# Infini-attention block, one core: a fifth stack slot, earlier stack loads, and a group's mixing, rounding and output products two steps later

## The chip, the core and the metric

The kernel runs on one core of a Trainium2 chip. Its engines work side by side, each on its own list of instructions in a fixed order: PE (TensorE, products; its weight loads are listed as PEld), DVE (VectorE), ACT (ScalarE), POOL (GpSimd) and SP (SyncE, which here only issues DMAs; its queue is shown as SPq). The metric is the device time of one execution in microseconds (us); three runs of the kernel before gave 816.80, 821.96 and 823.58, median 821.96.

## What is computed

One transformer block with conditioning: x is 2048 x 512, there are 32 heads of 16, 4 segments of 512 rows, and the hidden width of the feed-forward part is 1792.

```python
h = layernorm(x) * (1 + ca) + sa                       # sa, ca, ga, ... from silu(c) @ w_mod
# infini-attention on h, per segment s:
logits = qs @ ks.T * scale + mask                      # mask: -1e9 where key > query
a_dot = softmax(logits) @ vs
a_mem = (phi(qs) @ M) / (phi(qs) @ z + 1e-6)           # phi(t) = t + 1 if t > 0 else exp(t)
o = g * a_mem + (1 - g) * a_dot                        # g = sigmoid(beta), per head
M, z = M + phi(ks).T @ vs, z + sum(phi(ks))
x = x + ga * (o @ wo)
h = layernorm(x) * (1 + cb) + sb
x = x + gb * (gelu(h @ w1 + b1) @ w2 + b2)
```

## The kernel before

The program has three stages one after the other.

**Projections (0 to about 180 us).** q, k and v of all segments, and the memory terms of the heads. Parts of q and k in bf16 are stored in DRAM as QD and KD, the memory's share of the output (a_mem times its gate) as AMD, one tile of 128 x 512 per group. fp32 operands are split in a rounded high part and a low rest, and products are made of three terms.

**Attention (about 180 to 490 us).** The work is 64 steps (P) of two heads of one segment. Two steps make a *pair* (Q, 0 to 31; four heads), two pairs make a *group* (U, 0 to 15; eight heads), and four groups make a segment. The order of everything is written out by hand in the table PRM at the file's head: for every step a string of tokens tells in which order score maxima (S, function s_part, made for the step four ahead), the mask product of the smallest block (M, s_mask, once a pair), the transposed scores with their exponentials (T, st_part) and ten numbered places c0 to c9 come. Everything else is hung on such a place by a *position*: position p is place p % 10 of step p // 10. So 20 positions are one pair, 40 are one group, and the keys 'stacks', 'den', 'mix', 'ohi', 'olo', 'wo', 'ln' and so on hold positions, relative to the pair, the group or the segment.

What a pair goes through:

- load_stacks (L190 to L192, on SP) fills two tiles of 96 rows, kst and qst, with the bf16 parts of its four heads; there are four slots of such tiles, and pair Q uses slot Q % NK. Rows 96 to 127 hold ones; they are written once per slot by ACT (new_stack, L187). A load stands at position 20Q − 60.
- s_part makes scores on PE (L609) into one of six PSUM banks (att), DVE takes the masked maximum (L616). m_rows (POOL, L669) and m_put (PE L674 into the PSUM bank mm, ACT L131, a DMA that ACT issues, L677) write the maxima into rows 96 to 98 of qst.
- st_part makes transposed scores with the maxima subtracted (PE L644, L695), ACT takes the exponentials into pt (L714, L725), POOL zeroes what lies above the diagonal (L698).
- pv_part (PE L739) multiplies with V into the bank pvb, and pv_out copies it to ts (ACT L131) and stores it to DRAM (TD, SP L750).

What a group goes through after its second pair:

- pv_in (SP L755, L757, and L764, L769 for memory rows): loads back the denominators as dn (128 x 32), the numerators as opk (128 x 512), and amB from AMD.
- den: DVE takes the reciprocal of dn (L774); POOL, for the last segment DVE, scales it by 1 − g (L775); SP stores it as RD (L777). rb_in (SP L783) loads it back as rbB, spread over rows.
- mix: opk * rbB (L788), + amB (L790), on POOL for groups 0 to 12, else on DVE. o_hi: ACT rounds it to oh (L131). o_lo: the rest ol (L805).

When all four groups of a segment are there, wo_x loads the rows of x (L825), wo_part makes the *output products* (PE L816, 12 per 128 rows, into the bank mm), and wo_out adds x (DVE L834, or ACT copies to xo at L831 and POOL adds at L832) and stores X2D (SP L835). This takes four pairs, one block of rows each, and happens while the next segment's attention runs. For segment 0 the second layernorm follows (ln2_load L568, ln2_stats, ln2_rstd, ln2_apply on POOL at L156), and first_ht transposes it at the end of the stage (PE L161 in the bank mm, ACT L169, POOL L140). stage_w1 (SP L840) loads pieces of w1 as w1r; these take the buffers of the stack slots 0 and 1 (tag "wm").

**Feed-forward (about 490 to 817 us).** It begins with what is left of segment 3: groups 14 and 15 are mixed, and segment 3's output products are made between the first feed-forward products (L990). split_w1 (DVE L139, L140) splits the staged w1. gelu is on ACT (L993), the second products are at L1074.

Two queues matter for the change: SP issues its DMAs in program order and stands at each until its data and its buffer are there, and DVE, ACT and POOL each do likewise with their instructions.

The places of a group's parts, and of the loads, are hung on the table by these lines:

```python
ap(20 * Q + PRM["stacks"], load_stacks, Q)
...
ap(40 * U + PRM["mix"][z], mix, U)
...
ap(40 * U + PRM["ohi"][z], o_hi, U)
ap(40 * U + PRM["olo"][z], o_lo, U)
...
e = 160 * s + 230 + 20 * b
```

Of the kernel before, what the change touches and what calls it, by code (L numbers as in the profile page):

```python
# [8 lines left out]
F32 = mybir.dt.float32  # L9
# [15 lines left out]
PRM = {'order': ['S3 c0 S1 c1 c2 T0 c3 T2 S0 c4 c5 T4 S2 T3 c6 c7 M3 c8 c9 T1',  # L25
# [16 lines left out]
 'mput': [-14, -15, -13, -13],  # L42
 'mrow0': -19,
 'mput0': -9,
 'stacks': -60,
 'den': [84, 84, 84, 84],
 'dnl': 11,
 'rbl': 7,
 'mix': [105, 105, 100, 103],
 'ohi': [110, 110, 110, 111],  # L50
 'olo': [110, 110, 110, 116],
 'wo': [[2, 10, 10, 10], [6, 10, 11, 11], [2, 10, 10, 11]],
 'woout': [10, 11, 11],
 'wox': [-23, -23, -23, -13],
 'mixu': 13,
 'olou': 13,
 'htlo': 'p',
 'ht': 481,
 'htd': 20,
 'ln': [312, 339, 374, 408],  # L60
 'wl': [17, 66, 80, 81],
 'gate': 197,
# [21 lines left out]
 'lna': 'p',  # L84
 'mp': 0,
 'wout': ['vvvv', 'vava', 'vava'],
 'dens': ['p', 'p', 'p', 'v'],
 'pvo': ['a', 'a'],
 'mse': 'a',
 'w1at': [58, 59, 60],  # L90
 'mpre': 'a',
 'ohe': 'a',
 'pke': 'a',
# [12 lines left out]
def block_kernel(ctx: ExitStack, tc: tile.TileContext, x, wq, wk, wv, wo, betaq, betam,  # L106
                 w1, b1c, w2, b2, ccol, wmod, maskbd, mask8, out):
    nc = tc.nc
    v, act, pool, pe, sp = nc.vector, nc.scalar, nc.gpsimd, nc.tensor, nc.sync
# [19 lines left out]
    def copy(e, dst, src):  # L129
        if e == "a":  # L130
            act.activation(dst, src, AF.Copy)  # L131
        else:
            (v if e == "v" else pool).tensor_copy(dst, src)
# [43 lines left out]
    QD = [[dram.tile([6, 16, 8, 512], BF16, name=f"QD{s}_{g}") for g in range(4)] for s in range(NSEG)]  # L177
    KD = [[dram.tile([6, 16, 8, 512], BF16, name=f"KD{s}_{g}") for g in range(4)] for s in range(NSEG)]
    TERMS = {"q": (slice(0, 3), slice(4, 6), slice(3, 4)), "k": (slice(2, 5), slice(0, 6, 5), slice(1, 2))}
    NK = 4  # L180
    qst, kst = {}, {}

    def new_stack(i, pl=None):
# [5 lines left out]
    def load_stacks(Q):  # L189
        s, g, t = Q // 8, (Q // 2) % 4, Q % 2  # L190
        for st, dd in ((kst[Q % NK], KD), (qst[Q % NK], QD)):
            sp.dma_start(st[:96], dd[s][g].rearrange("c r e n -> (c r) e n")[:, 4 * t:4 * t + 4, :])  # L192
# [392 lines left out]
    so = sostack.enter_context(tc.tile_pool(name="so", bufs=2, reuse_waits="tile"))  # L585

    with ExitStack() as pb:
# [69 lines left out]
        def q_of(P, h, i):  # L657
            return qst[P // 2 % NK][:96, 2 * (P % 2) + h, 128 * i:128 * i + 128]

        def k_of(P, h, n):  # L660
            return kst[P // 2 % NK][:96, 2 * (P % 2) + h, 0:n]

# [9 lines left out]
        def m_put(Q):  # L672
# [3 lines left out]
            copy(PRM["mse"], ms, mm[:48, :128])  # L676
            act.dma_start(qst[Q % NK][96:99], ms)  # L677

# [14 lines left out]
        def st_mm(ps, P, h, j):  # L693
            q, k, e = qst[P // 2 % NK], kst[P // 2 % NK], 2 * (P % 2) + h
            pe.matmul(ps, k[:99, e, 128 * j:128 * j + 128], q[:99, e, 128 * j:512], start=True, stop=True)  # L695
# [56 lines left out]
        def pv_in(U):  # L752
            td = TD[U].rearrange("t (c r) n -> (t c) r n", r=32)
            dns[U] = so.tile([128, 32], F32, tag="dn", bufs=2, name=f"dn{U}")
            sp.dma_start(dns[U], td[:, 16, :])  # L755
            opks[U] = so.tile([128, 512], F32, tag="opk", bufs=2, name=f"opk{U}")
            sp.dma_start(opks[U], td[:, :16, :])  # L757
            if U < 15:
                am_in(U)

        def am_in(U):
            if U >= 4:
                am = so.tile([128, 512], F32, tag="xb" if U == 15 else "amB", bufs=3 if U == 15 else 1, name=f"amB{U}")
                sp.dma_start(am, AMD[U // 4][U % 4])  # L764
                opks[U, "am"] = am
                if U >= 12 and PRM["am3"]:
                    rm = so.tile([128, 512], F32, tag="rbB", bufs=2, name=f"rm{U}")
                    g = U % 4
                    sp.dma_start(rm, mem["r"][32 * g:32 * g + 8, :].unsqueeze(1).to_broadcast([8, 16, 512]))  # L769
                    opks[U, "rm"] = rm  # L770
# [78 lines left out]
        def at(P, part, f, *a):  # L849
            todo.setdefault((P, part), []).append((f, a))  # L850
# [23 lines left out]
        def ap(pos, f, *a):  # L874
            at(pos // 10, pos % 10, f, *a)

        for Q, P in ((2, -4), (3, -2)):
            at(P, 0, new_stack, Q, wop)
        for Q in range(2, 32):
            ap(20 * Q + PRM["stacks"], load_stacks, Q)  # L880
# [12 lines left out]
        for U in range(16):  # L893
            z = U // 4
            ap(40 * U + 20 + PRM["pvout"][z] + PRM["dnl"], pv_in, U)
            if U == 15:
                ap(40 * U + 20 + PRM["pvout"][z] + PRM["dnl"], am_in, U)
            ap(40 * U + PRM["den"][z], den, U)
            ap(40 * U + PRM["den"][z] + PRM["rbl"] + (5 if U == 14 else 0), rb_in, U)
            assert 20 + PRM["pvout"][z] + PRM["dnl"] <= PRM["den"][z] and PRM["den"][z] + PRM["rbl"] <= PRM["mix"][z]  # L900
            ap(40 * U + PRM["mmix"], mem_mix, U)
            ap(40 * U + PRM["mix"][z], mix, U)
            assert PRM["mmix"] <= PRM["mix"][z]
            ap(40 * U + PRM["ohi"][z], o_hi, U)
            ap(40 * U + PRM["olo"][z], o_lo, U)
            assert PRM["den"][z] <= PRM["mix"][z] <= PRM["ohi"][z] <= PRM["olo"][z]
        for s in range(NSEG):
            for b in range(4):
                e = 160 * s + 230 + 20 * b
                ap(e + PRM["wox"][s], wo_x, s, b)  # L910
                if s < 3:
                    assert PRM["wo"][s] == sorted(PRM["wo"][s]) and PRM["woout"][s] >= PRM["wo"][s][3]
                    for i, d in enumerate(PRM["wo"][s]):
                        ap(e + d, own, "mm", (s, b), wo_part, (s, b, i), False)
                    ap(e + PRM["woout"][s], own, "mm", (s, b), wo_out, (s, b), True)
        assert all(y[0] <= x <= y[3] < 0 for y in PRM["vl"] for x in y)
        assert PRM["wl"] == sorted(PRM["wl"]) and PRM["gate"] > PRM["wl"][1] + 60
        assert PRM["ln"][0] > 290 + PRM["woout"][0] and PRM["ln"][1] > PRM["ln"][0]
        assert PRM["ln"][1] + 3 * PRM["lnd"][0] < PRM["ln"][2] < PRM["ln"][3] and PRM["ht"] > PRM["ln"][3] + 3 * PRM["lnd"][1]
        def gate_load():  # L920
            sp.dma_start(gab, modD[5:6, :].to_broadcast([128, D]))
# [42 lines left out]
    with ExitStack() as pc:  # L964
# [127 lines left out]
        for n in range(AHEAD, NSEG * FB + AHEAD):  # L1092
            s, f = divmod(n, FB)
# [98 lines left out]
```

## Time and profile before

| | |
|---|---|
| runs | 816.80, 821.96, 823.58 us; median 821.96 |
| profiled execution | 818.88 us, of it span 817.1 us |
| mean granted TensorE clock | 0.992 |
| PE busy in the span | 97% |
| attention stage, 180 to 490 us | PE busy 294.35 of 310.00 us |
| feed-forward stage, 490 to 817 us | PE busy 323.34 of 327.00 us |

The profile's page gives the busy time of each engine and their shares in slices. Its trace answers finer questions: the windows give busy times, granted clock and DMA share of a stretch; the waits list for each engine what ended its idle time (engine, tile, line, what it waited for; total in us, how many times, the longest); the timeline lists single instructions with start and length, and in brackets the idle time before them with what ended it. Names such as "opk L788 <- DMA rbB<-RD" read: the instruction of line 788 that writes opk waited for the DMA from RD to rbB. Line numbers are those of the kernel before; the changed one has one line more, so its numbers are one higher from line 54 on.

### The profile page before, as it was taken

The page shows a single profiled execution, that of the slowest core. Times are in us where ns is not written, and L with a number is a line of the kernel's source. Part 1 is how long each engine was busy: PE and PEld are TensorE (multiplying, and loading weights), DVE is VectorE, ACT ScalarE, POOL GpSimd, SP SyncE. Part 2 cuts the span into 40 slices and gives each one's busy share as a digit, 9 for nine tenths or more (in the row PEclk, how much of TensorE's full clock was granted, in tenths as well). Part 3 has the DMA queues.
Part 4 walks back from the last instruction along what each step waited for, and adds up shares of the span by engine and source line. Part 5 has one row for each costly group of instructions (what it writes and reads, how often), then busy time and mean ns, then how long its engine had stood idle before and what let it go on. Part 6 is the DMA issues. An engine that isn't in the chain of part 4 may idle for free.

```text
span 817.1 us, 13438 instructions
## 1 busy us (share of the span) xinstructions
PE 793.3 (97%) x4637; PEld 549.9 (67%) x4637; DVE 499.8 (61%) x1341; ACT 364.5 (45%) x670; POOL 284.8 (35%) x508
## 2 busy tenths in 40 slices
PE   8999999999999899989989999999999999999998
PEld 4877777866434355445545548788888888888887
DVE  5686696559878777877777636885542353324223
ACT  3465545565778766666678662232211211211110
POOL 1347376541577545567768650000000000000000
PEclk9999999999999999999999999999999999999999
DMA  9597856495556666776657655633030111003001
GB/s 336 172 316 238 276 181 224 151 348 150 168 148 169 174 209 183 216 211 179 184 162 202 191 181 174 222 117 122 4 100 1 52 58 46 1 0 104 1 1 51
DMA packets 83565, 123.02 MB, mean 151 GB/s; under 512 B 14116, under 2 KB 46244, under 8 KB 82984
## 3 DMA queue, kind: packets, MB, share of 16 engines
q1 hardware_dynamic: 81000, 120.19, 46.9%
q10 hardware_dynamic: 2496, 1.97, 0.8%
q8 instruction: 36, 0.59, 0.3%
q14 instruction: 33, 0.27, 0.1%
HBM read 75.60 MB, written 46.15 MB: 149 GB/s over the span
## 4 chain that ended last, share of the span: by engine, by line
PE 43%; DMA 5%; POOL 3%; DVE 2%; issue 2%; ACT 1%; SPq 1%; DVEq 0%; POOLq 0%; ACTq 0%
PE acc L1074 17%; PE f1b L990 17%; PE pvb L739 2%; PE att L695 2%; PE att L609 2%; DMA RD<-dn 1%; DMA rbB<-RD 1%; PE mm L816 1%; POOL pt L698 1%; DMA xt<-X2D 1%; PE mm L161 1%; DMA opk<-TD 1%; DMA w2r<-in_w 1%; PE mm L1074 1%; POOL xt L156 1%
## 5 line engine op out<-in xcount | busy, mean ns | idle before, releaser
L616 DVE CUSTOM_DVE_ANT_0 dump<-att,maskb 128x512 bf16<-128x512 f32 (+2 forms) x384 | 192.1, 552 | 50.6 <-PE att L609 33.1
L714 ACT ACTIVATE pt<-att 128x512 f32<-128x512 f32 x256 | 144.1, 601 | 52.9 <-PE att L695 39.8
L993 ACT ACTIVATE gt<-f1b,b1t 128x512 f32<-128x512 f32 x56 | 38.5, 688 | 246.5 <-PE f1b L990 202.9
L139 DVE CAST gh<-gt 128x512 fp32r<-128x512 f32 x56 | 24.9, 446 | 165.9 <-ACT gt L993 165.9
L698 POOL TENSOR_SCALAR_AFFINE_SELECT pt<-pt 128x256 f32<-128x256 f32 x256 | 99.0, 409 | 52.4 <-ACT pt L714 31.4
L695 PE MATMUL att<-qst,kst 99*128 99x512 bf16 (+3 forms) x512 | 107.9, 304 | 1.9 <-ACT pt L714 1.6
L609 PE MATMUL att<-kst,qst 96*128 96x512 bf16 (+2 forms) x384 | 91.5, 331 | 8.8 <-DMA qst<-QD 7.4
L1074 PE MATMUL acc<-w2h,gh 128*128 128x512 f32 (+1 forms) x224 | 86.9, 388 | 0.0
L1074 PE MATMUL acc<-w2l,gh 128*128 128x512 f32 (+1 forms) x224 | 86.0, 384 | 0.4 <-DVE w2l L140 0.4
L1074 PE MATMUL acc<-w2h,gl 128*128 128x512 f32 (+1 forms) x224 | 85.7, 383 | 0.0
L739 PE MATMUL pvb<-pt,V 128*32 128x512 f32 (+2 forms) x992 | 82.7, 445 | 0.0
L695 PEld LDWEIGHTS <-kst 99*128 99x128 bf16 x512 | 44.6, 98 | 54.5 <-issue 31.7
L990 PE MATMUL f1b<-hodd,w1h 128*128 128x512 f32 x224 | 73.7, 390 | 0.0
L152 POOL TENSOR_SCALAR crs<-cmv 128x4 f32<-128x4 f32 x4 | 1.0, 247 | 173.0 <-DVE cmv L149 173.0
L609 PEld LDWEIGHTS <-qst 96*128 96x128 bf16 x384 | 33.4, 99 | 32.9 <-DMA qst<-QD 9.8
L739 PEld LDWEIGHTS pvb<-pt,V 128*32 128x32 f32 x992 | 25.1, 109 | 44.1 <-issue 40.1
L1074 PEld LDWEIGHTS acc<-w2l,gh 128*128 128x128 f32 x224 | 42.1, 188 | 9.2 <-DVE w2l L140 0.8
L990 PEld LDWEIGHTS f1b<-hodd,w1h 128*128 128x128 f32 x224 | 42.1, 188 | 8.6
L1074 PEld LDWEIGHTS acc<-w2h,gl 128*128 128x128 f32 x224 | 42.1, 188 | 8.3
L1074 PEld LDWEIGHTS acc<-w2h,gh 128*128 128x128 f32 x224 | 42.1, 188 | 8.2
L990 PE MATMUL f1b<-C0hh,w1l 128*128 128x512 f32 x112 | 43.9, 392 | 0.2 <-DVE w1l L140 0.2
L990 PE MATMUL f1b<-C0hh,w1h 128*128 128x512 f32 x112 | 44.0, 393 | 0.0
(214 smaller groups left out, 1544.5 us busy)
## 6 DMA issues: line engine op xcount, KB each, us to landing
kst<-KD SPq DMA_DIRECT2D x32, 384.0 KB
qst<-QD SPq DMA_DIRECT2D x32, 384.0 KB
TD<-ts SPq DMA_DIRECT2D x32, 256.0 KB
QD<-q SPq DMA_DIRECT2D x16, 384.0 KB
KD<-k SPq DMA_DIRECT2D x16, 384.0 KB
wm<-in_wmod SPq DMA_DIRECT2D x20, 256.0 KB
QD<-q SPq DMA_DIRECT2D x16, 256.0 KB
KD<-k SPq DMA_DIRECT2D x16, 256.0 KB
```

The costliest lines, as they stand in the source:

```text
L139: v.tensor_copy(hi, src)
L156: (e or v).tensor_scalar(xh[:, b, :], xt[:, b, :], t[1][:, b, 0:1], t[2][:, b:b + 1], op0=ALU.subtract, op1=ALU.mult)
L161: pe.transpose(ps[:, 128 * b:128 * b + 128], xh[:, b, 128 * d:128 * d + 128], ident)
L609: pe.matmul(ps, q_of(P, h, i), k_of(P, h, 128 * (i + 1)), start=True, stop=True)
L616: v.tensor_tensor_reduce(out=dump[n_dump[0] % 2][:, :n], in0=src, in1=maskb[:, 512 - n:], scale=-1.0, scalar=-4 * NEG, op0=ALU.add, op1=AL ...
L695: pe.matmul(ps, k[:99, e, 128 * j:128 * j + 128], q[:99, e, 128 * j:512], start=True, stop=True)
L698: pool.affine_select(out=t, in_=t, pattern=pattern, compare_op=ALU.is_ge, fill=0.0, base=0, channel_multiplier=-1)
L714: act.activation(pt[:, h, :], ps, AF.Exp, scale=0.25)
L739: pe.matmul(ps[32 * c:32 * c + 32, lo:hi], V[4 * s + j][:, VW * hd:VW * hd + 32], pt[:, c % 2, lo - o:hi - o], start=start, stop=stop)
L990: pe.matmul(ps, a[:, k, :], b[k], start=(i == 0), stop=(i == 11))
L993: act.activation(g, ps, AF.Gelu_apprx_tanh, bias=b1t[:, f:f + 1])
L1074: pe.matmul((mm if lo else acc[b])[:, lo:hi], a[:, c], w[:, lo:hi], start=(f == 0 and i == 0), stop=(last and i == 2))
```

## The change

The change makes five slots of stacks instead of four. The fifth is made at step 0 in its own pool. Loads of stacks stand a pair (20 positions) further up. Mixing stands 20 positions later for the groups of segments 0, 1 and 2 and 15 for those of segment 3; rounding (ohi) and rest (olo) 21 later, in segment 3 by 14; the output products with their loads of x and their sums 20 later for segments 0 to 2 (the new key 'wos'); the second layernorm of segment 0 20 later, its transposes ('ht') stay. w1 is staged four steps later. The scaling of the denominators goes to DVE for all groups. amB has two buffers.

```diff
- 'stacks': -60,
+ 'stacks': -80,
...
- 'mix': [105, 105, 100, 103],
- 'ohi': [110, 110, 110, 111],
- 'olo': [110, 110, 110, 116],
+ 'mix': [125, 125, 120, 118],
+ 'ohi': [131, 131, 131, 125],
+ 'olo': [131, 131, 131, 130],
...
+ 'wos': [20, 20, 20, 0],
...
- 'ln': [312, 339, 374, 408],
+ 'ln': [332, 359, 394, 428],
...
- 'dens': ['p', 'p', 'p', 'v'],
+ 'dens': ['v', 'v', 'v', 'v'],
...
- 'w1at': [58, 59, 60],
+ 'w1at': [62, 63, 64],
...
-    NK = 4
+    NK = 5
...
-                am = so.tile([128, 512], F32, tag="xb" if U == 15 else "amB", bufs=3 if U == 15 else 1, name=f"amB{U}")
+                am = so.tile([128, 512], F32, tag="xb" if U == 15 else "amB", bufs=3 if U == 15 else 2, name=f"amB{U}")
...
-        for Q, P in ((2, -4), (3, -2)):
+        for Q, P in ((2, -4), (3, -2), (4, 0)):
...
-                e = 160 * s + 230 + 20 * b
+                e = 160 * s + 230 + 20 * b + PRM["wos"][s]
...
-        assert PRM["ln"][0] > 290 + PRM["woout"][0] and PRM["ln"][1] > PRM["ln"][0]
+        assert PRM["ln"][0] > 290 + PRM["wos"][0] + PRM["woout"][0] and PRM["ln"][1] > PRM["ln"][0]
```

How this moves instructions is shown at three places. The first is SP at the start of the attention stage; kst and qst are the stacks with their slot's number, wor are pieces of wo. Before:

```order
L192 DMA kst2_2024<-KD0_1_90 96x2048
L192 DMA qst2_2023<-QD0_1_74 96x2048
L192 DMA kst3_2083<-KD0_1_90 96x2048
L192 DMA qst3_2082<-QD0_1_74 96x2048
L856 DMA wor0_2220<-in_wo 128x512
L192 DMA kst0_1781<-KD0_2_91 96x2048
```

Pair 4's load (from KD0_2) stands there behind the first piece of wo. In the changed kernel the same place reads:

```order
L193 DMA kst2_2024<-KD0_1_90 96x2048
L193 DMA qst2_2023<-QD0_1_74 96x2048
L193 DMA kst3_2085<-KD0_1_90 96x2048
L193 DMA qst3_2084<-QD0_1_74 96x2048
L193 DMA kst4_2154<-KD0_2_91 96x2048
L193 DMA qst4_2153<-QD0_2_75 96x2048
L857 DMA wor0_2225<-in_wo 128x512
L193 DMA kst0_1781<-KD0_2_91 96x2048
```

Pair 4 (the first of KD0_2) is loaded into its own slot ahead of wo, and slot 0 comes to pair 5. On ACT the constant rows of the fifth slot come between the last copy of V and the first exponentials; before:

```order
L131 ACTIVATE ms0_2119<-mm_1987 48x128
L677 DMA qst0_1780<-ms0_2119 3x16x128
L485 ACTIVATE V15_158<-pvb_2016 128x32x16
L714 ACTIVATE pt0_0_2157<-att3_2013 128x512
L714 ACTIVATE pt0_1_2160<-att4_2014 128x512
```

The exponentials follow the copy of V at once. In the changed kernel:

```order
L132 ACTIVATE ms0_2121<-mm_1987 48x128
L678 DMA qst0_1780<-ms0_2121 3x16x128
L486 ACTIVATE V15_158<-pvb_2016 128x32x16
L188 ACTIVATE kst4_2154<-one_67 32x2048
L715 ACTIVATE pt0_0_2162<-att3_2013 128x512
L715 ACTIVATE pt0_1_2165<-att4_2014 128x512
```

One instruction of ACT is new there.

The second place is PE and POOL where segment 1's last output products and segment 0's transposes meet (mm is the shared PSUM bank, xt2 the layernormed rows, pt the exponentials, opk9, rbB9 and amB9 the parts of group 9, xb the sum with x, C0hl the low part of a transposed tile). PE before:

```order
L609 MATMUL att3_2013<-kst2_2024,qst2_2023 128x256
L609 LDWEIGHTS qst2_2023
L609 MATMUL att3_2013<-kst2_2024,qst2_2023 128x256
L161 MATMUL mm_1987<-ident_63,xt2_0_3849 128x128 x4
L695 LDWEIGHTS kst0_1781
```

The transposes stand behind score products. In the changed kernel:

```order
L817 MATMUL mm_1987<-woh_2000,oh7_4379 128x512
L817 MATMUL mm_1987<-woh_2000,ol7_4381 128x512
L817 MATMUL mm_1987<-wol_2001,oh7_4379 128x512
L162 MATMUL mm_1987<-ident_63,xt2_0_3944 128x128 x4
L696 LDWEIGHTS kst4_2154
```

They stand right behind the output products there, which use the same bank. POOL before:

```order
L669 TENSOR_TENSOR nm0_2002<-nm0_2002 128x16 x2
L698 AFFINE_SELECT pt45_1_4670<-pt45_1_4670 128x2x128 x2
L788 TENSOR_TENSOR opk9_4482<-opk9_4482,rbB9_4643 128x512
L790 TENSOR_TENSOR opk9_4482<-opk9_4482,amB9_4484 128x512
L832 TENSOR_TENSOR xb1_3_4494<-xo1_3_4712,xb1_3_4494 128x512
L698 AFFINE_SELECT pt46_1_4723<-pt46_1_4723 128x2x128 x2
```

Three operations on 128 x 512 stand in a row. In the changed kernel:

```order
L670 TENSOR_TENSOR nm1_2003<-nm1_2003 128x16 x2
L699 AFFINE_SELECT pt47_1_4779<-pt47_1_4779 128x2x128 x2
L789 TENSOR_TENSOR opk9_4465<-opk9_4465,rbB9_4633 128x512
L791 TENSOR_TENSOR opk9_4465<-opk9_4465,amB9_4467 128x512
L833 TENSOR_TENSOR xb1_3_4601<-xo1_3_4825,xb1_3_4601 128x512
L141 TENSOR_TENSOR C0hl0_0_4836<-C0h0_0_4833,C0hh0_0_4835 128x512
L699 AFFINE_SELECT pt48_1_4839<-pt48_1_4839 128x2x128 x2
```

Group 9 is mixed behind step 47's exponentials instead of step 45's, with the first low part of the feed-forward tiles behind it.

The third place is SP at the end of the attention stage (TD, dn, opk, amB, rm, RD, rbB with a group's number; w1r are pieces of w1). Before, from the store of group 14's first half:

```order
L750 DMA TD14_5512<-ts28_5513 128x512
L840 DMA w1r4_5547<-in_w1 128x4x128 x2
L835 DMA X2D2_123<-xb2_2_5342 128x512
L777 DMA RD13_5570<-dn13_5450 128x32
L783 DMA rbB13_5594<-RD13_5570 128x1x512
L750 DMA TD14_5512<-ts29_5614 128x512
L835 DMA X2D2_123<-xb2_3_5471 128x512
L755 DMA dn14_5656<-TD14_5512 128x1x32
```

The last piece of w1 (w1r4) stands ahead of the second store of TD14. In the changed kernel, from that second store on:

```order
L751 DMA TD14_5487<-ts29_5594 128x512
L841 DMA w1r0_5614<-in_w1 128x4x128 x2
L836 DMA X2D2_123<-xb2_2_5451 128x512
L756 DMA dn14_5635<-TD14_5487 128x1x32
L758 DMA opk14_5637<-TD14_5487 128x1x512
L765 DMA amB14_5639<-AMD3_2_119 128x512
L770 DMA rm14_5641<-rdd3_1972 128x1x512
L841 DMA w1r2_5660<-in_w1 128x4x128 x2
L751 DMA TD15_5681<-ts30_5682 128x512
L841 DMA w1r4_5704<-in_w1 128x4x128 x2
L836 DMA X2D2_123<-xb2_3_5561 128x512
L778 DMA RD14_5722<-dn14_5635 128x32
```

All three pieces of w1 were issued before that store; they stand behind it now, and group 14's reciprocal rows (RD14) stand behind them and behind the last store of X2D.

## The prediction, made before the changed kernel ran

> **What bounds the kernel now.** I read four views in this order: the page's busy times, the windows by stage, the waits of TensorE, and then the timeline around each of these waits. The profiled execution took 818.88 us, 817.1 of it span; it lies 3.1 below the median of the three runs, 821.96.
>
> First the page's line of busy times, then the windows of the three stages (start and end, length, busy time of PE, PEld, DVE, ACT and POOL, granted clock, DMA share, GB/s):
>
> ```profile
> PE 793.3 (97%) x4637; PEld 549.9 (67%) x4637; DVE 499.8 (61%) x1341; ACT 364.5 (45%) x670; POOL 284.8 (35%) x508
> ```
>
> ```profile
> 0.00:180.00 180.00, 175.63 (x833) 130.23 (x834) 120.40 (x220) 95.56 (x167) 87.21 (x108) 1.00 0.73 246
> 180.00:490.00 310.00, 294.35 (x2325) 151.55 (x2324) 232.41 (x852) 212.20 (x418) 190.95 (x393) 0.98 0.63 185
> 490.00:817.00 327.00, 323.34 (x1482) 268.17 (x1481) 146.95 (x270) 56.74 (x86) 6.68 (x8) 1.00 0.20 66
> ```
>
> TensorE sets the end. The change removes no product, so only its idle time and its clock can be won. The attention stage, 180 to 490 us, holds 310.00 − 294.35 = 15.65 us of idle PE; the feed-forward stage has 3.66 in 327 and no place for a gain. Which waits those are is in the waits of PE (total, times, longest):
>
> ```profile
> PE att L609 <- DMA qst<-QD: 7.4, 6, 2.8
> PE att L644 <- ACT pt L714: 2.2, 1, 2.2
> PE att L739 <- POOL pt L698: 1.9, 1, 1.9
> PE att L695 <- ACT pt L714: 1.6, 2, 1.2
> PE mm L674 <- POOL nm L669: 0.8, 1, 0.8
> PE att L609 <- ACT pt L714: 0.6, 1, 0.6
> ```
>
> They sum to 14.5 of the 15.65. The first row is stack loads that land too late. The others look like ACT's and POOL's own slowness; the timeline of the longest, at 425 us, tells otherwise:
>
> ```profile
> 425.64 1.28 POOL L788 TENSOR_TENSOR opk<-opk,rbB 128x512 f32<-128x512 f32 x1 [3.74 <-DMA rbB<-RD]
> 428.29 0.63 ACT L131 ACTIVATE oh<-opk 128x512 fp32r<-128x512 f32 x1 [2.46 <-POOL opk L790]
> 429.46 0.26 PE L644 MATMUL att<-kst,qst 96*128 96x128 bf16 x1 [2.22 <-ACT pt L714]
> ```
>
> POOL stands 3.74 us for the reciprocal rows (rbB) of a group, ACT's rounding (oh) stands 2.46 us for POOL, the exps queued behind it on ACT are late, and PE stands 2.22 us for them. The origin is a DMA here too. Both DMAs go through SP, which issues in order; its rows for one group of two pairs, the first store of the next two groups, and the ACT instruction that made the last one's data:
>
> ```profile
> 253.53 0.38 SPq L750 DMA_DIRECT2D TD<-ts  x1
> 260.01 0.60 SPq L755 DMA_DIRECT2D dn<-TD  x1
> 264.18 0.34 SPq L777 DMA_DIRECT2D RD<-dn  x1
> 269.04 0.60 SPq L783 DMA_DIRECT2D rbB<-RD  x1
> 271.15 0.38 SPq L750 DMA_DIRECT2D TD<-ts  x1
> 284.14 0.60 ACT L131 ACTIVATE ts<-pvb 128x512 f32<-128x512 f32 x1 [0.65 <-PE pvb L739]
> 288.04 0.40 SPq L750 DMA_DIRECT2D TD<-ts  x1
> ```
>
> The cycle TD store to TD store takes 271.15 − 253.53 = 17.6 us, because SP stands twice for a round trip through DRAM. Two pairs take PE 15.06 us where it doesn't wait, by the mask product that comes once a pair:
>
> ```profile
> 209.35 0.38 PE L653 MATMUL att<-maskb,identb 128*128 128x512 bf16 x1
> 216.88 0.38 PE L653 MATMUL att<-maskb,identb 128*128 128x512 bf16 x1
> ```
>
> (7.53 each). So where no output products lengthen the pairs, groups 1 to 6, SP falls behind by up to 2.5 us a group, until PE waits for it; the store at 288.04 stands 3.30 us after its data were ready (284.14 + 0.60).
>
> The second loss is the clock. The windows around four of the waits, and around a fifth for comparison (same columns):
>
> ```profile
> 230.00:240.00 10.00, 8.13 (x58) 3.12 (x59) 6.24 (x25) 6.38 (x13) 5.75 (x11) 0.83 0.69 198
> 285.00:295.00 10.00, 7.85 (x68) 3.91 (x68) 6.60 (x25) 5.74 (x12) 4.36 (x10) 1.00 0.69 193
> 345.00:360.00 15.00, 13.24 (x98) 5.63 (x96) 11.46 (x45) 9.40 (x19) 8.57 (x17) 0.89 0.71 215
> 425.00:440.00 15.00, 12.78 (x111) 6.96 (x108) 10.27 (x40) 10.37 (x21) 11.83 (x21) 0.89 0.60 173
> 480.00:495.00 15.00, 13.01 (x88) 7.00 (x87) 5.86 (x11) 7.36 (x13) 5.09 (x10) 0.89 0.45 146
> ```
>
> Lost clock is 0.17 × 10 = 1.7 us once and 0.11 × 15 = 1.65 three times, together 6.65. Idle and clock make 22.3 us that could be won at most. The 2.76 us gap at 287 had no slow clock behind it, the 1.87 us one at 234 had, so I count half clock only where the windows show it.
>
> **The change, part by part**, against 818.88.
>
> (1) *Fifth stack slot, loads one pair earlier.* A load is issued two pairs ahead of its first score product instead of one, 7.53 us more, against a longest wait of 2.8. With five slots the slot's last reader stands as far ahead of the load as it did with four, so SP doesn't stand longer for it. What goes is 7.4 and the half clock at 234, 1.7: 9.1. SP is still up to 3.3 late in groups 1 to 6, so I leave 1.0: **−8.1** (−9.1; −4.6 if half of it stays).
>
> (2) *Mixing, rounding and output products one pair later* (segments 0 to 2). What it must cover:
>
> ```profile
> POOL opk L788 <- DMA rbB<-RD: 20.6, 8, 5.4
> DVE opk L788 <- DMA rbB<-RD: 9.8, 1, 9.8
> SPq L783 <- DMA RD<-dn: 44.0, 15, 5.7
> SPq L764 <- POOL opk L790: 6.5, 5, 2.9
> ```
>
> The longest lateness in POOL's row, 5.4, is less than a pair. So PE's rows by way of ACT and POOL go: 2.2 + 1.6 + 0.8, without the 0.6 that I leave with the rest, 4.6, and two half clocks, 3.3: **−8.0** (−8.0; −4.0 if half stays). The output products move with the mixing, so they don't wait for it. The second buffer of the memory rows frees SP's 6.5; without it, mixing later would hold the next group's load. Off PE's path: 0.
>
> (3) *The end of the stage.* Group 13's mixing is on DVE and stood 9.8 us (row above), its rounding stood ahead of the last exps on ACT, and PE lost the 1.9 of the third wait row and 1.65 of clock near 487. Mixing moves by 1.5 steps and the rounding by 1.4, behind those exps; the nine or more products of segment 2's last output then stand there too. **−3.0** (−3.55 to 0).
>
> (4) *The denominators' scaling from POOL to DVE* for twelve groups:
>
> ```profile
> L775 DVE TENSOR_SCALAR dn<-dn,omg x4: 241/284/398, 453.2 to 500.4; 128x32 f32<-128x32 f32 x4
> ```
>
> 12 × 0.284 = 3.4 us more on DVE, which is busy 232.41 of the stage's 310 and has the cover; the store of RD no longer goes by way of POOL's queue, which shortens SP's cycle. **0** (0 to +3.4 if DVE has no slack where it stands).
>
> (5) *Constant rows of the fifth stack*, written by ACT right ahead of the first exps. The row of their kind, and what stands at that place:
>
> ```profile
> L187 ACT ACTIVATE kst<-one x4: 1887/1904/1904, 162.4 to 189.4; 32x2048 bf16<-32x2048 f32 x4
> 197.51 1.08 ACT L714 ACTIVATE pt<-att 128x512 f32<-128x512 f32 x2
> 201.16 0.38 PE L695 MATMUL att<-qst,kst 99*128 99x512 bf16 x1 [0.43 <-ACT pt L714]
> ```
>
> PE already waits 0.43 for ACT there, so the full 1.90 shows: **+1.9** (0 to 3.6, with a half clock).
>
> (6) *Output products of segment 1 now stand right ahead of the transposes of segment 0*, which use the same PSUM bank. The copy that empties the bank:
>
> ```profile
> 403.69 0.39 PE L816 MATMUL mm<-wol,oh 128*128 128x512 f32 x1
> 404.12 0.60 ACT L831 ACTIVATE xo<-mm 128x512 f32<-128x512 f32 x1 [1.79 <-PE mm L816]
> ```
>
> From the end of the last product, 404.08, to the end of the copy is 0.64, and a signal: **+0.8**, at the one place where the two meet (0.8; 2.5 with a half clock).
>
> (7) *w1 staged four steps later*, because slots 0 and 1, whose buffers it takes, now serve the last two pairs. Before, its first load left SP 26.1 us ahead of its split:
>
> ```profile
> 458.87 0.38 SPq L840 DMA_DIRECT2D w1r<-in_w  x1
> 478.14 0.40 SPq L750 DMA_DIRECT2D TD<-ts  x1
> 484.99 0.42 DVE L139 CAST w1h<-w1r 128x512 fp32r<-128x512 f32 x1
> ```
>
> Now it leaves right behind the store that stood at 478.14, 6.9 us ahead. A transfer of this kind took at most 6.5 us, from the TD store at 253.53 to the load at 260.01 that stood for it, so w1 is just in time. SP's reciprocal rows of group 14 stand behind w1 and an X2D store, too. **+1.0** (0; 4.1 if it takes 11 us, by two of SP's longest stands for such a trip, 5.7 each).
>
> (8) *POOL has four 128x512 operations in a row* where output, mixing and first feed-forward tile meet, 4 × 1.28 = 5.1 us instead of 3.8; the causal zeroing behind it, and so PE, is later: **+1.0** (0 to 2).
>
> Sum: −8.1 − 8.0 − 3.0 + 1.9 + 0.8 + 1.0 + 1.0 = **−14.4**, 804.5 by the profiled run. As that run lies 3.1 below the median of the runs, I set the forecast halfway: **806.0 us**.
>
> **The rivals.** (A) SP stays the limit. Later mixing and earlier loads leave SP's cycle at 17.6 us against 15.06, and it is just behind later. Six groups times 1.7 (the mean of 1 and 2.5) is 10.2; the pair that was won, 7.5, takes this up, 2.7 remain and two half clocks, 3.35: 806.0 + 6.1 = **812**. For it: SPq's 44.0 us. Against it: the store of RD is no longer behind POOL.
>
> (B) The other side: DVE takes the wait. The reciprocal is on DVE, in order, ahead of the masked maxima that empty PE's score banks. If SP's lateness moves from the loads onto the rows that it reads, DVE stands in each of groups 1 to 7, and PE with it: 7 × (2.8, the longest wait that SP's lateness has cost PE, + 1.65) = 31.2, so 806.0 + 31.2 = **837**. It decides once these rows are later than DVE's slack, a quarter of a pair (232.41 of 310 busy), 1.9 us. For it: SP was 3.3 late at 288. Against it: the denominators keep their place, and none of PE's waits goes back to them now.
>
> (C) The clock doesn't hang on these gaps: all 6.65 stays, 806.0 + 6.65 = **812.6**. The gap of 2.76 without, and of 1.87 with half clock speak for it; that all four windows lie at one of the waits speaks against it. The Trainium skill, "TensorE: Matmul & The Clock Gate", Part 1 on the clock gate, says that the clock falls to half after an idle window of some 3.4 us in a window that runs freely. No gap here is that long and the clock fell at 1.87, so the trace agrees only if the window counts thin work around a gap as idle; read so, its rule gives this rival's time, read as written it gives no half clock at all.
>
> (D) The change doesn't do what it says: only loads get on time by half (−4.6), mixing only moves its wait to the output products behind it, and parts 5 to 8 are paid, +4.7: 818.9 + 0.1 + 1.5 = **820.5**. Against it: 7.53 us of lead over 5.4.
>
> **How the numbers follow.** The forecast has 0.64, A 0.18, B, C and D 0.06 each. All terms at their good ends give 804.5 − 5.5 = 799.0, and the lowest of the three runs, 816.80, lies 2.1 under the profiled one: 797. All terms half way to their bad ends give 806.0 + 10.7 = 816.7, and A and C lie below that. Outside are B, D and a small rest, under 0.2: range **797 to 817**. A measurement here can tell about 1% from no change, that is under 813.7: faster 0.61 (of the forecast) + 0.12 (of A) + 0.04 (of C) = 0.77, slower 0.06 (B), within 0.17.
>
> **What would show it.** Right: PE's row for qst from DRAM is under 1.5 us and POOL's for rbB under 5; the windows at the four places have clock 1.00 and the stage's PE idle is under 6 us; ACT's constant rows stand ahead of the first exp, with a PE wait near 2 behind it; a PE gap near 0.8 at the first transpose. Wrong: a DVE row for dn in microseconds (B), SP stores more than 3 us behind their data in groups 1 to 6 with PE waiting for exps (A), slow clock without a gap before it (C), output products waiting for ol or oh (D), or a loss in the feed-forward stage, where f1b would wait for w1 or for segment 0's tiles.

## The result, and the profile after

| | before | after | ratio, 95% interval |
|---|---|---|---|
| median | 823.17 us | 810.16 us | 0.9887 [0.9852, 0.9922] |
| the same kernel once more, on another occasion | 818.96 us | 809.79 us | 0.9885 [0.9857, 0.9913] |
| profiled execution (span) | 818.88 (817.1) | 815.29 (813.4); once more 809.67 (807.8) | |

The change makes the kernel 1.1% faster, some 9.4 us. The direction was forecast, the size (14.4 us) was not reached. The first profiled execution after is the longest of its five runs, 815.29; the second, 809.67, lies at the median, so sizes are read from the second and places from both. Kernels are compared by their ratios to runs of before on the same chip, since the median of before itself lies between 818 and 823 on the different occasions; so the ratio of the first row is not the quotient of the two medians beside it (0.984).

First the page's busy line and PE's waits after (first execution; total, times, longest):

```profile
PE 790.9 (97%) x4637; PEld 549.1 (68%) x4637; DVE 505.9 (62%) x1353; ACT 366.1 (45%) x671; POOL 282.7 (35%) x496
```

```profile
PE att L696 <- DMA qst<-ms: 5.4, 6, 1.5
PE att L696 <- DVE nm L617: 3.3, 1, 3.3
PE acc L817 <- ACT oh L132: 2.1, 1, 2.1
...
PE f1b L991 <- DVE w1h L140: 0.8, 1, 0.8
PE mm L817 <- ACT ms L132: 0.8, 1, 0.8
...
PE mm L162 <- ACT xo L832: 0.7, 1, 0.7
```

The row for stack loads (7.4) is gone, as are the rows behind exps that mixing delayed. New rows stand in their place. The largest, "qst<-ms", is a DMA that the prediction did not name: the 12 KB of score maxima that ACT sends into rows 96 to 98 of qst (L678), and for which the transposed scores wait.

Where the time went is read from windows cut at the same instructions in every kernel: the starts of the mask products of pairs 0, 2, 13, 18 and 30, and the first feed-forward product. Before, from pair 0 on without the stretch 13 to 18 (start and end, length, busy time of PE, PEld, DVE, ACT, POOL, granted clock, DMA share, GB/s):

```profile
187.37:202.26 14.89, 14.14 (x81) 9.10 (x81) 13.93 (x55) 7.87 (x14) 2.44 (x8) 1.00 0.44 123
202.26:291.68 89.42, 83.23 (x706) 37.79 (x704) 71.53 (x275) 66.70 (x137) 54.89 (x125) 0.98 0.57 163
...
341.27:457.47 116.20, 109.61 (x882) 57.55 (x880) 88.17 (x325) 79.61 (x158) 83.05 (x156) 0.97 0.63 185
457.47:489.65 32.18, 30.19 (x237) 15.18 (x234) 14.05 (x40) 21.51 (x43) 19.70 (x38) 0.96 0.61 184
489.65:817.13 327.48, 323.69 (x1484) 268.51 (x1482) 146.95 (x270) 56.92 (x86) 6.93 (x8) 1.00 0.20 66
```

After, second execution:

```profile
186.07:202.94 16.87, 14.41 (x81) 9.05 (x80) 14.27 (x55) 9.81 (x15) 2.44 (x8) 1.00 0.59 149
202.94:290.35 87.41, 82.75 (x707) 38.26 (x705) 72.39 (x278) 66.55 (x137) 54.84 (x123) 0.98 0.55 157
...
339.67:445.38 105.71, 103.71 (x870) 54.08 (x868) 90.62 (x329) 79.30 (x158) 81.14 (x151) 1.00 0.67 196
445.38:477.90 32.52, 30.93 (x248) 17.12 (x246) 13.64 (x39) 22.36 (x45) 20.76 (x40) 1.00 0.56 163
477.90:807.76 329.86, 324.15 (x1482) 267.93 (x1482) 148.56 (x273) 56.43 (x85) 7.49 (x8) 1.00 0.21 69
```

The same stretches for the kernels that matter, each from its own profiled execution (lengths in us). That of the loads alone, 823.17, lies 3.5 above the median of its runs; that of the later mixing alone, 815.38, lies 2.1 below.

| stretch | before | after | after again | loads alone | late alone | loads halved |
|---|---|---|---|---|---|---|
| to pair 0 | 187.37 | 186.70 | 186.07 | 184.77 | 184.21 | 186.20 |
| pairs 0, 1 | 14.89 | 17.86 | 16.87 | 17.86 | 14.89 | 16.87 |
| pairs 2 to 12 | 89.42 | 85.87 | 87.41 | 92.79 | 94.20 | 82.28 |
| pairs 13 to 17 | 49.59 | 49.67 | 49.32 | 49.30 | 49.31 | 49.33 |
| pairs 18 to 29 | 116.20 | 109.64 | 105.71 | 116.31 | 107.38 | 106.99 |
| to the feed-forward stage | 32.18 | 32.51 | 32.52 | 28.81 | 34.46 | 32.52 |
| feed-forward stage | 327.48 | 331.12 | 329.86 | 331.60 | 329.21 | 328.64 |

A pair with output products takes 10.06 us (302.04 to 312.10 before, by its mask products), one without 7.53. Where mixing is late, twelve output products, 10.06 − 7.53 = 2.5 us, have moved from pairs 18 to 29 into the next row (882 products against 870). So from before to the second execution the gain is 116.20 − 105.71 − 2.5 = 8.0 in pairs 18 to 29 and 32.18 − 32.52 + 2.5 = 2.2 behind them; pairs 2 to 12 give 2.0, pairs 0 and 1 lose 2.0, the feed-forward stage loses 2.4. Not all of the 8.0 is the mixing's. PE's wait for stack loads had a part in pairs 18 to 29, too; the row of the waits in that window before:

```profile
PE att L609 <- DMA qst<-QD: 1.5, 2, 1.0
```

So the loads, the largest term of the prediction, brought some 3.8 of 8.1 (2.0, 0.3 in pairs 13 to 17, and 1.5), and lost 2.0 of it again in pairs 0 and 1; the mixing brought about what was forecast.

### The profile page after: what moved, and what is told of

It reads as the page before. It is cut to its first block, busy times and chain, and to the rows that moved or that the text cites. A ratio compares the mean times of both kernels' runs of the same rounds, so it can differ in the third digit from the quotient of the medians.

```text
span 813.4 us, 13418 instructions
## 1 busy us (share of the span) xinstructions
PE 790.9 (97%) x4637; PEld 549.1 (68%) x4637; DVE 505.9 (62%) x1353; ACT 366.1 (45%) x671; POOL 282.7 (35%) x496
## 4 chain that ended last, share of the span: by engine, by line
PE 47%; DVE 2%; DMA 2%; ACT 1%; issue 1%; SPq 0%; POOL 0%; DVEq 0%
PE acc L1075 18%; PE f1b L991 17%; PE pvb L740 3%; PE att L696 3%; PE mm L817 3%; PE att L610 2%; PE mm L162 1%; DMA xt<-X2D 1%; DMA w2r<-in_w 1%; DMA rm<-rdd 1%; PE mm L1075 1%; DVE dump L617 0%; DVE xb L835 0%; DVE cst L149 0%; ACT pt L715 0%
```

## The experiments

Each kernel was timed in five rounds beside the kernel before. The theory at first, M: each part of the change takes away its own waits, and new waits gave some back. The rivals are named in each expectation.

**The loads alone** (the kernel before with the fifth slot):

```diff
- 'stacks': -60,
+ 'stacks': -80,
- 'w1at': [58, 59, 60],
+ 'w1at': [62, 63, 64],
-    NK = 4
+    NK = 5
-        for Q, P in ((2, -4), (3, -2)):
+        for Q, P in ((2, -4), (3, -2), (4, 0)):
```

> The kernel before with the fifth slot and the loads a pair earlier alone (w1 is staged four steps later, since its buffers are in use longer). Theory M, each part removes its own waits: PE's row for qst from DRAM (7.4 us) and its half clock go, but the constant rows ahead of the first exps cost 1.5 to 5 and the small DMA of the maxima, which now stands on PE's path, some 4; mixing's waits stay: 818 to 824 us. Rival R, SP's lateness was one cause for all and the loads cure it: 812 or less, with POOL's row for rbB far under 20.6.

Measured: 819.68 us, ratio 1.0012 [0.9987, 1.0037]. This is M's number. PE's waits:

```profile
PE att L695 <- DMA qst<-ms: 6.1, 4, 2.2
PE att L695 <- ACT pt L714: 5.3, 4, 2.4
```

The loads' row is gone and the time is not: PE now stands for the small DMA and for exps behind mixing, whose rbB row on POOL is still 23.4. Rival R falls.

**The later mixing alone** (four slots, loads as before; mix, ohi, olo, wos, ln and amB as in the change):

```diff
- 'mix': [105, 105, 100, 103],
+ 'mix': [125, 125, 120, 118],
...
- 'ln': [312, 339, 374, 408],
+ 'ln': [332, 359, 394, 428],
```

> The kernel before with mixing, rounding, rest, output products and second layernorm later and two amB buffers; four slots, loads as before. Theory M: PE's waits for exps behind mixing go (4.6 and two half clocks) and so does the one at the end of the stage, the loads' 7.4 stays, and the layernorm's statistics ahead of the maxima on DVE cost 3.3 and a half clock: 813 to 818 us. Rival R: nothing, 821 to 824.

Measured: 817.48 us, ratio 0.9993 [0.9965, 1.0022]. By its ratio it makes no difference, as the rival had it (in us it lies at the end of M's range, since before itself was 818.78 on this occasion); but its profile shows two effects that cancel. PE's first wait, and pairs 18 to 29:

```profile
PE att L610 <- DMA qst<-QD: 13.2, 9, 3.0
```

```profile
342.61:449.99 107.38, 104.11 (x871) 54.11 (x869) 87.96 (x324) 79.66 (x159) 83.36 (x158) 1.00 0.66 199
```

Pairs 18 to 29 are 8.8 shorter (6.3 without the moved products), clock 1.00 instead of 0.97; pairs 2 to 12 are 4.8 longer, and PE stands 13.2 for the loads instead of 7.4. So M falls as well: the parts don't add up. Either one hands its wait to the other; only both together bring 1.1%.

**Who makes pairs 0 and 1 longer? The constant rows on POOL** instead of ACT:

```diff
-        act.activation(kst[i][96:].rearrange("p e n -> p (e n)"), one[96:].to_broadcast([32, 2048]), AF.Copy)
+        o = (kst[i][96:].rearrange("p e n -> p (e n)"), one[96:].to_broadcast([32, 2048]))
+        pool.tensor_copy(*o) if i == 4 else act.activation(*o, AF.Copy)
```

> The changed kernel with the constant rows of the fifth slot written by POOL, which has nothing else to do there, instead of ACT. Theory: the wait of 1.51 us at the first exps and the 6.8 us of half clock behind it (3.4 lost) go: 3 to 5 us under the changed kernel's profiled run, 806 to 808 against its median of 810. Rival: that half clock was of the profiled execution alone or comes without the wait, and the time stays within 1 us of 810.

Measured: 808.58 us, ratio 0.9877 [0.9853, 0.9901], not told apart from the change. Pairs 0 and 1 still take 16.84. So the theory falls: the wait is still there, and its releaser is not ACT:

```profile
197.96 0.61 PE L697 MATMUL att<-qst,kst 99*128 99x512 bf16 x3 [1.78 <-DMA qst<-ms]
```

**Pair 4's load held back.** The constant rows on POOL reach over 32 rows of the load too, so that it must wait for them:

```diff
+        lo = 64 if i == 4 else 96
+        o = (kst[i][lo:].rearrange("p e n -> p (e n)"), one[lo:].to_broadcast([128 - lo, 2048]))
+        pool.tensor_copy(*o) if i == 4 else act.activation(*o, AF.Copy)
```

> The changed kernel with the fifth slot's constant rows written by POOL over 32 rows more, so that pair 4's load into that slot has to wait for them, to about 199 us instead of 186. Theory: the wait of 1.4 us at the first transposed scores comes from that load, 768 KB in flight when the small DMA of pair 0's maxima is issued, and not from the constant rows; it goes, pairs 0 and 1 together take 15 us again instead of 16.9, and the time falls by 1 to 2. Rival: the wait stays, another transfer is in its way.

Measured: 811.81 us, ratio 0.9914 [0.9884, 0.9944]. The mechanism holds, the gain doesn't. The load's issue on SP, and PE's two gaps:

```profile
198.20 0.30 SPq L195 DMA_DIRECT2D kst<-KD  x1
```

```profile
199.83 0.59 PE L698 MATMUL att<-qst,kst 99*128 99x512 bf16 x3 [0.43 <-ACT pt L717]
204.55 0.61 PE L698 MATMUL att<-qst,kst 99*128 99x512 bf16 x3 [2.70 <-DMA qst<-ms]
```

With no load in flight, pair 0's maxima are in time and pairs 0 and 1 take 14.88; now the load, issued at 198.20, meets pair 1's maxima, which are sent at 198.40, and PE stands 2.70 for these. Pairs 2 to 12 take 91.18 instead of 87.41, so that nothing is left of the gain.

**The denominators' scaling back on POOL:**

```diff
- 'dens': ['v', 'v', 'v', 'v'],
+ 'dens': ['p', 'p', 'p', 'v'],
```

> The changed kernel with the denominators' scaling of groups 0 to 11 back on POOL. Theory: mixing has a pair of slack now, so it makes no difference, 809 to 811. Rival 1: the scaling on DVE delays the maxima and costs up to 3.4, so 806 to 808. Rival 2: SP stands longer for POOL and the loads are late again, 813 or more.

Measured: 810.37 us, ratio 0.9893 [0.9872, 0.9915]: no difference from the change (0.9885), as expected.

**The change again:**

> The changed kernel once more, for the other runs to stand beside and for a second profiled execution. If the half clocks at 199 and 353 us of the first one belong to the program, they are there again; if they are of that execution, the span is nearer 808 and at least one is gone.

Measured: 809.79 us, its profile shown above. The half clocks at 199 and 353 of the first execution are absent; one of 3.41 us at 283 is there. So where a half clock falls belongs to the execution.

**The end of the attention stage:** RD14 ahead of the last X2D store and the last piece of w1.

```diff
- 'w1at': [62, 63, 64],
+ 'w1at': [62, 63, 65],
-            ap(40 * U + PRM["den"][z], den, U)
+            ap(40 * U + PRM["den"][z] - (5 if U == 14 else 0), den, U)
```

> The changed kernel with group 14's denominators five places earlier and the last piece of w1 one step later, so that SP issues RD14 ahead of the last store of X2D and of that piece. Theory: the 2.1 us that PE waits for group 15's rounding in the feed-forward stage go, 1.5 to 2.5 less than the changed kernel. Rival: group 15's own round trips through DRAM set it, and it stays.

Measured: 808.79 us, ratio 0.9878 [0.9838, 0.9917], not told apart. PE's wait stayed (2.1 and 0.9 in the two executions of the change):

```profile
PE acc L817 <- ACT oh L132: 2.7, 1, 2.7
```

and this is why, on SP:

```profile
472.73 0.38 SPq L778 DMA_DIRECT2D RD<-dn  x1
...
477.23 0.34 SPq L751 DMA_DIRECT2D TD<-ts  x1
479.33 0.60 SPq L784 DMA_DIRECT2D rbB<-RD  x1
483.62 0.58 SPq L756 DMA_DIRECT2D dn<-TD  x1
...
488.35 0.32 SPq L778 DMA_DIRECT2D RD<-dn  x1
493.01 0.59 SPq L784 DMA_DIRECT2D rbB<-RD  x1
```

Group 14 is early, and group 15 still goes through three round trips behind its own TD store, 477.23 to 493.01 and on to PE at 498.9. The rival holds.

**The layernorm's statistics a step later:**

```diff
- 'ln': [332, 359, 394, 428],
+ 'ln': [332, 369, 404, 440],
```

> The changed kernel with the second layernorm's statistics of segment 0 one step later, and what follows them too; its load stays. Theory: DVE no longer stands for the load ahead of the maxima, PE's wait at 353 us (3.3) and the half clock go: 1 to 4 less than the changed kernel, and DVE's row for xt is under 0.5 at that place. Rival: other work holds the maxima up there, and the wait stays.

Measured: 809.79 us, ratio 0.9890 [0.9860, 0.9920]: nothing won, and DVE's row for xt is still 2.0. The load lands later than I had thought, and in the second execution of the change PE's gap there is 0.81, behind the small DMA, not 3.26 behind DVE; the long one was of the first execution.

**Segment 0's maxima put earlier:**

```diff
- 'mput': [-14, -15, -13, -13],
+ 'mput': [-17, -15, -13, -13],
```

> The changed kernel with segment 0's maxima put into their rows three places earlier (position -17 instead of -14). Theory: the small DMA of the maxima (12 KB) lands 5 to 6.6 us after its issue because stack loads are in flight, and 4.7 us is all it had; with some 1.2 us more PE's row for qst from ms falls from 5.4 to under 2.5, and the time by 2 to 4. Rival: PE then stands at the put for POOL's rows, and nothing is won.

Measured: 809.94 us, ratio 0.9893 [0.9858, 0.9927]. PE's row for the small DMA falls as forecast, and nothing is won, for another reason than the rival's. PE, then DVE:

```profile
PE att L696 <- DVE nm L617: 2.2, 3, 1.2
PE att L696 <- DMA qst<-ms: 1.9, 2, 1.2
```

```profile
DVE dn L775 <- DMA dn<-TD: 8.1, 5, 1.8
```

The wait went to the maxima on DVE, which stands for the next DMA.

**Both, with the denominators later:**

```diff
- 'mput': [-14, -15, -13, -13],
+ 'mput': [-17, -15, -13, -13],
- 'den': [84, 84, 84, 84],
+ 'den': [92, 88, 84, 84],
```

> The changed kernel with segment 0's maxima put three places earlier (as in the run of that alone) and the denominators of segments 0 and 1 eight and four places later, so that DVE does not stand for them ahead of the maxima. Theory: in the run of the earlier put alone the wait went from the small DMA (1.9 left) to DVE, which stood 8.1 us for dn; with that under 4, the two together take 804 to 807. Rival: pairs 5 to 12 take 63 us again, with yet another wait, and the time stays at 808 to 811.

Measured: 812.20 us, ratio 0.9926 [0.9888, 0.9963]. DVE's row for dn falls to 3.2 and pairs 2 to 12 take 84.32, but pairs 0 and 1 take 18.83 and the feed-forward stage 332.95. The expected gain isn't there.

**What paces pairs 2 to 12? SP's order spread out**, so that it seldom stands for a round trip:

```diff
- 'den': [84, 84, 84, 84],
- 'dnl': 11,
- 'rbl': 7,
+ 'den': [97, 92, 91, 84],
+ 'dnl': [21, 21, 21, 11],
+ 'rbl': [5, 5, 5, 7],
```

> The changed kernel with SP's order for the groups of segments 0 to 2 spread out: a group is loaded back one TD store after its own, its reciprocal rows are loaded one stack load and one TD store after RD's store (dnl 21, den 97, 92, 91, rbl 5). Nothing is left out. Theory A: in pairs 2 to 12, which have gained nothing by the change (87 us from pair 2 to 13, of 80 at 7.3 a pair), SP's stands for round trips set the pace; SP's rows for RD and TD fall from 53 and 43 us to under 30 together, those pairs take 82 to 84, and the time falls by 3 to 6. Rival D: the small DMA of the maxima sets it, its row stays above 4, and so does the time. Rival L: what is won there is lost by later mixing, a POOL row for rbB comes back.

Measured: 817.45 us, ratio 0.9988 [0.9966, 1.0011]; all of the gain is lost. SP's stands for the two round trips in the change (second execution), then here, then PE's row and pairs 2 to 12 here:

```profile
SPq L784 <- DMA RD<-dn: 52.3, 16, 6.0
SPq L756 <- DMA TD<-ts: 41.0, 13, 6.5
```

```profile
SPq L784 <- DMA RD<-dn: 21.5, 13, 4.8
...
SPq L756 <- DMA TD<-ts: 2.1, 1, 2.1
```

```profile
PE att L696 <- DMA qst<-ms: 10.3, 6, 2.5
```

```profile
204.78:291.82 87.04, 82.95 (x706) 38.12 (x704) 72.25 (x278) 66.60 (x137) 55.14 (x124) 0.98 0.55 163
```

SP's stands for the two round trips fall from 93 to 24 us, in pairs 2 to 12 from 40.4 to 0.2, and the stretch takes 87.04 instead of 87.41. In all SP stands there as long as before (75.2 against 74.5), now for DVE's denominators, ACT's copies and stacks that PE still reads. The round trips don't pace the stretch: theory A falls. PE's wait for the small DMA more than doubles (4.3 to 10.3).

**Half of the bulk:** stack loads from pair 5 on cut to 48 rows, which leaves out part of the scores.

```diff
-            sp.dma_start(st[:96], dd[s][g].rearrange("c r e n -> (c r) e n")[:, 4 * t:4 * t + 4, :])
+            n = 96 if Q < 5 else 48
+            sp.dma_start(st[:n], dd[s][g].rearrange("c r e n -> (c r) e n")[:n, 4 * t:4 * t + 4, :])
```

> The changed kernel with the stack loads from pair 5 on cut to 48 of their 96 rows (384 KB a pair instead of 768); the rows left out keep an older pair's numbers, so it leaves out part of the scores, with every instruction of PE, DVE, ACT and POOL as before. Theory D: the small DMA of the maxima is late because of the bulk in flight, and that is what holds pairs 5 to 12: PE's row for qst from ms falls from 4.3 to under 2, all in pairs 0 and 1, pairs 5 to 12 take 60 to 62 us instead of 63 to 65, and the time falls to 804 to 807. Rival A: SP's round trips hold them, which bring other data: both stay, 809 to 811.

Measured: 804.74 us, ratio 0.9826 [0.9803, 0.9850]. PE's row, SP's two rows, and pairs 2 to 12:

```profile
PE att L697 <- DMA qst<-ms: 2.3, 3, 1.3
```

```profile
SPq L785 <- DMA RD<-dn: 44.7, 16, 5.0
SPq L757 <- DMA TD<-ts: 41.5, 13, 7.2
```

```profile
203.07:285.35 82.28, 80.80 (x707) 37.75 (x704) 72.47 (x278) 66.16 (x137) 54.81 (x123) 1.00 0.49 123
```

Pairs 2 to 4, whose loads are whole, take 21.99 here and in the change (second execution), by their mask products; pairs 5 to 12 take 60.29 instead of 65.42, as theory D had it. Of these 5.1 us, 1.9 are PE's busy time, since no half clock falls there, and 3.2 are waits; with the constant rows on POOL, where none falls either, pairs 5 to 12 take 63.52. SP's two rows fall a little as well (86 against 93, in pairs 2 to 12 33.1 against 40.4), but the spread order took them away altogether and won nothing. So what holds these pairs is DMA traffic that makes other transfers late: PE's row for the small one falls in pairs 2 to 12 from 2.1 to 0.9 (over the kernel to 2.3, not under 2), and DVE's for the denominators from 3.4 to 0.4. How much each of the two costs is not separated. And stack loads are not the only traffic: one small DMA still took 6.28 us here, from 274.96 to 281.24.

No kernel that computes everything is told apart from the change on the better side; the two lowest, 808.58 and 808.79, lie within its interval by their ratios, 0.9877 and 0.9878.

## Why the prediction was right in direction and too large

- **(1) Loads a pair earlier, −8.1.** The row "qst<-QD" left PE's list as forecast. The failed step is "What goes is 7.4 and the half clock": I left 1.0 for what stays late, on SP. The runs show that the wait moved to a transfer that took 5.0 to 6.6 us under bulk where PE waited for it, and had 3.6 to 5.8. Pairs 2 to 12 gave 2.0 in the second execution and 3.6 in the first, pairs 18 to 29 another 1.5; alone the loads lengthen pairs 2 to 12 by 3.4, in an execution with more half clock.
- **(2) Mixing a pair later, −8.0.** In the second execution 8.0 in pairs 18 to 29, with 1.5 of (1) and the 0.7 of (6) inside, so 7.2; in the first 116.20 − 109.64 − 2.5 = 4.1 instead of 8.0, since it has a gap of 3.26 there, behind DVE's layernorm statistics, and a half clock. POOL's row for rbB (20.6) is gone. The mechanism was right; the size lies within its bounds in the second execution, and below them in the first (4.1 − 1.5 + 0.7 = 3.3). One small slip: of the 1.6 that the sum takes from PE's waits for exps, 0.43 is the wait at 201 that (5) quotes; nothing is mixed yet there, so mixing later could not remove it.
- **(3) The end of the stage, −3.0.** 2.2: PE's wait of 1.9 and the half clock near 487 are gone. With the loads alone, where mixing stays, both are gone too, and PE has no wait in that stretch (28.81); so that group 13's mixing is their cause is not shown.
- **(4) Scaling on DVE, 0.** Shown by the run with POOL.
- **(5) The constant rows, +1.9.** The size was right by luck, +2.0 to +3.0, and the cause wrong. ACT had the cover; pair 4's load, issued at 187 instead of 203, made the maxima late. I had counted what the moved load frees and not what it meets. In the first execution a half clock followed as well.
- **(6) Transposes behind output products, +0.8.** The row says 0.7.
- **(7) w1 later, +1.0 of 0 to 4.** The feed-forward stage is 2.4 longer (3.6 in the first execution). The place was named, the mechanism was another. f1b waits 0.8, but not for w1's transfer: DVE splits w1 right behind the rest ol of group 13, for which it stood 2.56 behind ACT's rounding (second execution):

```profile
476.05 1.36 DVE L806 TENSOR_TENSOR ol<-opk,oh 128x512 fp32r<-128x512 f32 x1 [2.56 <-ACT oh L132]
477.34 0.41 DVE L140 CAST w1h<-w1r 128x512 fp32r<-128x512 f32 x1
```

```profile
477.90 0.47 PE L991 MATMUL f1b<-C0hh,w1h 128*128 128x512 f32 x1 [0.79 <-DVE w1h L140]
```

  With the later mixing alone, w1 staged as before, the same product waits the same 0.79. So this is a price of the later rounding, for which (3) left 0.55 at most (3.55 less 3.0). The wait "acc <- oh", for group 15's rounding, is up to 2.9 in the executions of the change and its variants; it is 2.2 with the loads and w1 alone, and absent with the later mixing alone, so it comes with w1's or the loads' new places. From the stretch ahead of the feed-forward stage to the end, (3) and (7) together bring nothing: 32.18 + 327.48 = 359.66 before, 32.52 + 329.86 − 2.5 = 359.88 after.
- **(8) Four operations of POOL in a row, +1.0.** PE's list has no row for POOL's mixing or its causal zeroing: 0.

The windows add up: +2.0 − 2.0 − 0.3 − 8.0 − 2.2 + 2.4 and −1.3 before pair 0, where the change moves nothing, make −9.4, the difference of the two spans. Against −14.4, term (1), with 2.0 + 0.3 + 1.5, is short by 4.3, (3) by 0.8, and (7) and (5) cost 1.5 more; (2), (6) and (8) were −6.2 in the forecast and are −6.5, and the 1.3 was not in it: it is luck. One of the prediction's own signs shows the miss: PE's idle time from pair 0 to the feed-forward stage was to fall under 6 us, and went from 15.7 to 10.7.

Of the rivals, A named the stretch that gained little, but its cause, SP's round trips, is refuted by the run with SP's order spread out. B's 837 did not come, though its mechanism is there: DVE does stand for dn, 3.3 us in the first execution after, 4.5 in the second and 8.1 with earlier maxima. In the second execution PE pays for it at one place, and the half clock at 283 follows. DVE, then PE:

```profile
280.32 0.35 DVE L775 RECIPROCAL dn<-dn 128x32 f32<-128x32 f32 x1 [2.43 <-DMA dn<-TD]
```

```profile
281.62 0.32 PE L696 MATMUL att<-qst,kst 99*128 99x384 bf16 x1 [1.58 <-DVE nm L617]
```

C is refuted. Three executions (loads halved; constant rows on POOL; statistics later) have no half clock but in the last 2 us of the span, with gaps up to 1.78 us, and the second of the change has 1.7 us of loss, where C kept 6.65. In the first execution after, the clock fell at the gaps of 1.51 and 3.26:

```profile
199.77:206.60 6.83, 6.77 (x27) 3.18 (x25) 5.58 (x22) 4.60 (x10) 2.92 (x9) 0.50 0.02 4
353.37:356.78 3.41, 3.41 (x16) 1.22 (x18) 2.84 (x10) 1.92 (x4) 0.60 (x1) 0.50 0.70 198
```

D is refuted for the whole; its time, no gain, is that of either part alone.

What stays open: which of the late transfers would be next if the maxima were sent by another way, and why the spread order cost 7 us more in pairs 18 to 29 (112.78) than the change; its waits there are for the small DMA, 2.38 and 2.51, and I have not tried it with earlier maxima.

## What to carry to other kernels

A wait for a late load is a term of the sum only if nothing else is nearly late at the same place: before crediting it, list for each product the other transfers that it needs, with the time each has and the time it takes under the load's own traffic. Two changes that each hand their wait to the other are worth nothing alone and something together, so test both singly and jointly. Halving the bytes, with every instruction kept, tells a busy DMA from a queue that stands: the pairs with whole loads kept their time, the others took 5 us less, and the queue's stands stayed within a tenth of what they were.

## What the runs showed of the hardware

A DMA of 12 KB was not fast here for being small. The rows of DMA issues (how many, KB each), of the small one and of one of the two that load a stack:

```profile
kst<-KD SPq DMA_DIRECT2D x32, 384.0 KB
...
qst<-ms ACTq DMA_DIRECT2D x32, 12.0 KB
```

Before, pair 0's maxima were there at the latest 3.46 us after their issue; with pair 4's stack load issued 16 us earlier the same product waited until 5.14 after it. The issue and the product, of before and then of after:

```profile
193.63 1.35 ACTq L677 DMA_DIRECT2D qst<-ms  x1
```

```profile
197.09 0.38 PE L695 MATMUL att<-qst,kst 99*128 99x512 bf16 x1
```

```profile
192.96 1.36 ACTq L678 DMA_DIRECT2D qst<-ms  x1
```

```profile
198.10 0.55 PE L696 MATMUL att<-qst,kst 99*128 99x512 bf16 x2 [1.51 <-DMA qst<-ms]
```

That the load is the cause is shown by the run that holds it back, where pair 0's product doesn't wait for the maxima. This happens where the 16 DMA engines are busy 0.56 to 0.59 of the time on average (pairs 0 and 1 after; 0.44 before), and the small DMA is issued on another engine's queue than the bulk. The Trainium skill's page "TensorE: Matmul & The Clock Gate", Part 1, gives the clock's window as some 3.4 us; the trace agrees in length, with stretches of 3.41 us and twice that, 6.83, at half clock. Its rule asks for an idle window; here the clock fell at gaps of 1.51 and 3.26 us in the first execution of the change and at 1.58 in the second, and did not at one of 1.78 (constant rows on POOL).
